# Banded attention and a feed-forward block: a second place for float32 queries and keys, and new due times for the attention units

## The chip, the core and the metric

The kernel runs on one core of a Trainium2 chip as one program. The metric is the device time of one execution in microseconds; of the kernel before there are three runs with a median of 982.79 us, and one more execution taken by the hardware profiler. Most executions of one kernel agree within 0.3%.

## The reference

Eight batches of 576 positions, eight heads of 64. Heads 0 to 3 attend to the 32 positions up to their own, heads 4 to 7 to every fourth of the 128 positions up to their own. The attention's output is then normalised, multiplied up to 2048 columns, clipped at zero, multiplied back to 512 and added to what went in:

```python
scores = np.where(masks, (q @ k.T) / 8, -1e9)      # two bands, by head
attn = exp(scores - max); attn /= attn.sum(-1) + 1e-9
x = (attn @ v) as (batch, seq, 512)
xn = (x - mean) / sqrt(var + 1e-6) * g
out = x + maximum(xn @ w1, 0) @ w2                  # 512x2048, 2048x512
```

## The kernel before, in words

**Tiles and blocks.** The 4608 rows are 36 tiles of 128 rows; three tiles make a block, and there are twelve blocks. Tiles 0 to 3 go through an early form of attention in float32, while the weights are still being loaded. Every later tile t goes through these units, each with a letter in the plan:

- L, `load_tile`: queries and keys as float32 into `qk32` (two DMAs of 512 KB, since each half of the partitions gets its own copy, L179) and values into `v32` (L187). Both places are single (`bufs=1`).
- A, `attn_prep`: splits the float32 values into a high and a low float16 part: casts on ACT (L301, L272, L151) and subtractions on POOL (L302, L273) and on DVE (L152). The halves lie in a `slot`, one of five equal places of 8 KB per partition (`SLOTS`, L245) that the raw weights and the early values use as well. A tile's slot is read until the value products of the tile after it (L513 takes `old`).
- S, `attn_scores`: 24 matmuls (L323), eight for the plain heads, then sixteen for the dilated ones, with the mask added by DVE between them (L341, L355), since `ps_s` is a single place in PSUM.
- M, `attn_softmax`: maximum on DVE (L437), subtraction on POOL (L439), two exponentials on ACT (L444, L445), the low part on POOL (L446), 18 transposes on DVE (L451, L425, L427, L428).
- V, `attn_values`: 40 matmuls (L521; 24 in a tile that begins a batch), then 1/sum and the output x on DVE (L527, L531, L533).
- N and T: mean and variance on DVE (L542), the power on POOL (L547), the normalised tile on DVE (L556), its two halves on ACT and POOL (L561, L562), and two transposing DMAs (L569) into the block's `xT`. There are two of these, one of which lies in the tile `w1_sb`: in the profile it is called `xT` for even blocks and `w_sb` for odd ones.

**The feed-forward block** (`ffn`). "Up" are 16 groups of 12 matmuls with 384 columns (L590), each ended by a clip on ACT (L596) and a difference on DVE (L597); "down" are three tiles of 48 matmuls with 512 columns (L613), each ended on DVE (L619) and by a DMA to the output (L627). Blocks 0 and 1 are worked tile by tile with matmuls of 128 columns. A block's first up matmul needs the T of all its three tiles.

**What sets the order.** All work of all tiles is cut into units with a due time. A unit may not be due before those it is built on, a table (`MOVED`) sets some times by hand, and the units are written out sorted by due time (L834). For tiles from 6 on, the time of A is `t_at = max(t_at + GAP, start - AHEAD - PER_TILE * (NB - 1 - i))`, where `start` is the time of the tile's block: `AHEAD` says how long before its block the last tile of it is prepared. S, M, V and T follow A by 6, `SOFTMAX`, `VALUES` and `READY`, and L follows the A of the tile before. The layer that records the program then keeps each engine's instructions in about that order, but lets one go ahead that it takes to be ready sooner. What stands on an engine is run in that order: an instruction that waits holds up all behind it on its engine. All DMAs are issued by SP, in one queue, and a DMA that waits for its place to become free holds up those behind it too.

Of the kernel before, what the change touches and what calls it, by code (L numbers as in the profile page):

```python
# [10 lines left out]
F32 = mybir.dt.float32  # L11
# [6 lines left out]
P = 128  # L18
H = 8
HP = 4  # L20
D = 64
# [10 lines left out]
NQK = 2 * HP * P  # L32
NBLK = NT // NB
EARLY = 4
AHEAD = 45.0
GAP = 10.0
SOFTMAX, VALUES, READY = 10.0, 20.0, 28.0
CW, SLOTS = 2, 5
HG = 4
SUMS = 128  # L40
# [7 lines left out]
}  # L48

MOVED = {  # L50
# [6 lines left out]
}  # L57
APART = 2

# [7 lines left out]
def attention_then_ffn(ctx: ExitStack, tc, qkv, masks, g, w1, w2, out):  # L67
# [3 lines left out]
    work = ctx.enter_context(tc.tile_pool(name="work", bufs=2))  # L71
# [87 lines left out]
    def after_weights():  # L159

        raw = state.get("raw")
        return nullcontext() if raw is None else tc.issue_after(raw)

    def load_tile(t):
        with after_weights() if t < NB * 2 else nullcontext():
            load_tile_now(t)

    def load_tile_now(t):
        if t == 0:
            state["early"] = work.tile([P, 2, 2, HP, P], F32, name="qk32", bufs=1)  # L170
        if t < EARLY:
            qk32 = state["early"][:, t % 2]
            nc.sync.dma_start(out=qk32, in_=qkv[t, :, 0:NQK])
            q32, k32 = qk32[:, 0], qk32[:, 1]
        else:
            qk32 = work.tile([P, 2, 2, HP, P], F32, name="qk32", bufs=1)
            src = qkv[t, :, 0:NQK].rearrange("(a d) e -> d a e", a=2)
            for on in (slice(0, D), slice(D, P)):
                nc.sync.dma_start(out=qk32[on].rearrange("d a x h c -> d a (x h c)"), in_=src)  # L179
            q32, k32 = qk32[:, :, 0], qk32[:, :, 1]  # L180
        if t < EARLY:
            v32 = slot().bitcast(F32)[:, 0 : 16 * (D + 1)]
            state[t] = dict(q32=q32, k32=k32, v32=load_ranges(t, v32))
        else:
            v32 = work.tile([P, H, D], F32, name="v32", bufs=1)
            v_in = qkv[t, :, NQK:].rearrange("p (h d) -> p h d", h=H)
            state["load", t] = nc.sync.dma_start(out=v32, in_=v_in).ins  # L187
            state[t] = dict(q32=q32, k32=k32, v32=v32)
# [54 lines left out]
    def slot():  # L243

        return work.tile([P, CW * DM * 2], I32, name="slot", bufs=SLOTS)  # L245

    def room_of(t):

        st = state[t]
        x = slot().bitcast(F16)  # L250
        at = 0
        for name, *shape in (("qs", H, P), ("khp", HP, W + P), ("klp", HP, W + P), ("khd", HP, P), ("kld", HP, P), ("vl", H, D)):
            n = shape[0] * shape[1]
            st[name] = x[:, at : at + n].rearrange("p (h c) -> p h c", h=shape[0])
            at += n
# [26 lines left out]
    def split_last(t):  # L282

        st = state[t]
        st["v32"] = work.tile([P, H, D], F32, name="v32", bufs=1)
        nc.sync.dma_start(out=st["v32"], in_=qkv[t, :, NQK:].rearrange("p (h d) -> p h d", h=H))
        for x in pt_a + pt_d:
            nc.gpsimd.memset(x, 0.0)
        room_of(t)
        kh, kl = st["khp"], st["klp"]  # L290
        halves_of(st["k32"], kh[:, :, W:], kl[:, :, W:])
        st.update(kh=kh, kl=kl)
        prep_v(t)
# [441 lines left out]
    units = {}  # L735

    def unit(name, when, what, *after):

        when = MOVED.get(name, when)
        for a in after:  # L740
            if a in units:
                when = max(when, units[a][0] + 0.001)
        units[name] = (when, len(units), what)
        return when

    PER_TILE = 24.0
    for fg in range(NKC):
        unit(f"C{fg}", TIMES["C"][fg], lambda fg=fg: prep_w1(fg), f"C{fg - 1}")
        unit(f"s{fg}", TIMES["C"][fg] + 5.0, lambda fg=fg: split_w1(fg), f"C{fg}", f"s{fg - 1}")
# [10 lines left out]
    for b in range(NBLK):  # L760
        blk = dict(t0=b * NB, b=b)
        for i in range(NB):
            t = b * NB + i
            if t < EARLY:
                t_at = TIMES["E"][t]
                if t:
                    unit(f"L{t}", t_at - 8.0, lambda t=t: load_tile(t), f"V{t - 2}")
                else:
                    unit("L0", 0.5, load_first)
                for n, (name, what) in enumerate((  # L770
                    ("S", scores_early), ("M", softmax_early), ("V", values_early), ("N", norm),
                )):
                    unit(f"{name}{t}", t_at + 3.0 * n, lambda t=t, what=what: what(t), f"L{t}", f"{name}{t - 1}")
                unit(
                    f"T{t}", t_at + 10.0, lambda t=t, i=i, blk=blk: transposes(t, blk, i), f"N{t}",
                    f"P{NFC // NW2 - 1}" if b else None,
                )
                if t == EARLY - 1:
                    unit(f"A{t}", TIMES["X"], lambda t=t: split_last(t), f"v{t}", f"N{t}")
                continue  # L780
            if t - EARLY < len(TIMES["t"]):
                t_at = TIMES["t"][t - EARLY]
            else:
                t_at = max(t_at + GAP, start - AHEAD - PER_TILE * (NB - 1 - i))

            def do(name, when, what, *after):
                return unit(f"{name}{t}", t_at + when, lambda t=t: what(t), f"{name}{t - 1}", *after)

            unit(f"L{t}", units[f"A{t - 1}"][0] + 1, lambda t=t: load_tile(t), f"A{t - 1}")


            t_at = do("A", 0, attn_prep, f"L{t}", f"V{t - 2}")
            if t % TPP == 5 and t + 4 < NT:
                do("v", 2, scale_later, f"A{t}")
            do("S", 6, attn_scores, f"A{t}")
            do("M", SOFTMAX, attn_softmax, f"S{t}", f"V{t - 1}")
            do("V", VALUES, attn_values, f"M{t}")
            do("N", VALUES + 2, norm, f"V{t}")
            unit(
                f"T{t}", t_at + READY, lambda t=t, i=i, blk=blk: transposes(t, blk, i),  # L800
                f"N{t}", f"P{NFC // NW2 - 1}" if b else None, f"b{b - 2}",
            )
        ups, downs = ffn(blk, b < APART)
        if b < APART:
            for i in range(NB):
                t = b * NB + i
                when = TIMES["U"][t] if t < len(TIMES["U"]) else start
                for fq in range(NKC):
                    us = ups[(4 * i + fq) * 4 // HG : (4 * i + fq + 1) * 4 // HG]
                    when = unit(  # L810
                        f"U{t}.{fq}", when, lambda us=us: [what() for _, what in us],
                        f"T{t}", f"s{fq}", f"U{t}.{fq - 1}", f"U{t - 1}.{fq}", f"D{t - 1 - i}.{fq}",
                    )
                    when += sum(took for took, _ in us)
                if b == 0:
                    when = TIMES["D"] + 10.4 * i
                for p in range(NKC):
                    took, what = downs[4 * i + p]
                    when = unit(
                        f"D{t}.{p}", when, what,  # L820
                        f"P{(4 * p + 3) // NW2}", f"U{t}.{p}", f"D{t}.{p - 1}", f"D{t - 2}.3" if p == 0 else None,
                    )
                    when += took
                start = max(start, when) if b else start
            last = tuple(f"D{t}.{NKC - 1}" for t in range((b + 1) * NB))
            units[f"b{b}"] = (max(units[a][0] for a in last), len(units), lambda: None)
        else:
            when = max(start, units[f"T{b * NB + NB - 1}"][0] + 0.1, max(units[a][0] for a in last))
            for n, (took, what) in enumerate(ups + downs):
                name = f"b{b}" if n == len(ups) + len(downs) - 1 else f"b{b}.{n}"  # L830
                when = unit(name, when, what, f"T{b * NB + NB - 1}", f"b{b}.{n - 1}", *last) + took
            last = (f"b{b}",)
            start = max(start + PER_TILE * NB, when)
    for _, _, what in sorted(units.values(), key=lambda e: e[:2]):  # L834
# [72 lines left out]
```

## Time and profile before

| | |
|---|---|
| three runs, median (lowest, highest) | 982.79 us (981.22, 983.58) |
| the profiled execution, its time | 991.04 us |
| its span, first to last instruction | 989.3 us |
| busy: PE, DVE, POOL, ACT | 910.8, 640.4, 313.3, 311.1 us |
| mean granted TensorE clock | 0.974 |
| HBM traffic over the span | 82 GB/s |

PE is TensorE's matmuls, PEld its weight loads, DVE VectorE, ACT ScalarE, POOL GpSimd, SP the engine that issues the DMAs. Times in the profile are microseconds from the first instruction. The granted clock is a share of full speed. A row of the groups or of the timeline has the line of the code, the engine, the operation, the tile written and the tiles read, and how many. In a row of the windows, each engine has its busy time in that stretch with its instructions in brackets, then come the clock and the DMA engines' share. Matmuls are pipelined, so "busy" says that PE had work, not that it was fast. A number in square brackets is idle time before an instruction, with what ended it.

### The profile page before, as it was taken

To read this page: it belongs to the slowest core of one execution; us is meant where nothing else is said; L and a number is where in the kernel's file an instruction comes from. 1 tells how busy PE (TensorE), PEld (TensorE's weight loads), DVE (VectorE), ACT (ScalarE), POOL (GpSimd) and SP (SyncE) were. 2 spreads that over 40 slices of the span, in tenths; PEclk is the share of its full clock that TensorE was granted. 3 is DMA by queue.
4 is the path that set the end of the run, shared out by engine and by line. 5 is a ranking of instruction groups with operands and counts; after the bars stand their busy time and mean duration, and the time that the engine had idled before them with its cause. 6 is when DMAs were issued, how large, how long until landed. Compare 5 with 4: busy or idle time off the path is not lost.

```text
span 989.3 us, 18584 instructions
## 1 busy us (share of the span) xinstructions
PE 910.8 (92%) x7608; PEld 561.4 (57%) x7608; DVE 640.4 (65%) x1379; ACT 311.1 (31%) x588; POOL 313.3 (32%) x319
## 2 busy tenths in 40 slices
PE   4497887979999999899899899899999899999998
PEld 3387564777564655555565565465565465555553
DVE  4897648697575686675675685585585595585210
ACT  3655733242231531232231441141231241130110
POOL 1101454554233153253343162262432352120000
PEclk9998899989999999999999999999999999999999
DMA  7976654745514553252422642433703331200000
GB/s 231 353 230 151 161 121 109 131 77 119 100 31 94 136 111 65 57 117 64 103 51 59 163 102 54 76 76 67 142 13 86 77 68 34 46 17 28 22 1 32
DMA packets 79622, 93.39 MB, mean 94 GB/s; under 512 B 47920, under 2 KB 53680, under 8 KB 79536
## 3 DMA queue, kind: packets, MB, share of 16 engines
q1 hardware_dynamic: 79536, 92.21, 39.9%
q8 instruction: 59, 0.97, 0.4%
q14 instruction: 27, 0.22, 0.1%
HBM read 71.86 MB, written 9.44 MB: 82 GB/s over the span
## 4 chain that ended last, share of the span: by engine, by line
PE 55%; DMA 14%; DVE 11%; POOL 8%; ACT 6%; issue 4%; SPq 1%; POOLq 0%; ACTq 0%; DVEq 0%
PE ps_f L613 28%; PE ps_f L590 22%; DMA qk<-in_qkv 6%; POOL slot L273 3%; PE ps_v L521 3%; PE ps_s L323 3%; DVE pt_d L428 2%; POOL slot L302 2%; DMA xT<-xh 2%; DMA slot<-in_w 2%; DVE pt_a L425 1%; DMA v<-in_qkv 1%; DVE sc L355 1%; POOL pk L446 1%; DVE hl L597 1%
## 5 line engine op out<-in xcount | busy, mean ns | idle before, releaser
L590 PEld LDWEIGHTS <-w_sb 128*128 128x128 f16 x3072 | 264.4, 102 | 154.2 <-issue 13.9
L613 PE MATMUL ps_f<-w_sb,hh 128*128 128x512 f16 x1152 | 346.7, 381 | 3.5 <-ACT w_sb L151 3.2
L590 PE MATMUL ps_f<-xT,w_sb 128*128 128x384 f16 (+1 forms) x1536 | 206.7, 296 | 15.3 <-DMA xT<-xh 15.0
L613 PE MATMUL ps_f<-w_sb,hl 128*128 128x512 f16 x576 | 219.3, 381 | 0.0
L590 PE MATMUL ps_f<-w_sb 128*128 128x384 f16 (+1 forms) x1536 | 204.1, 295 | 8.0 <-DMA w_sb<-xh 7.7
L613 PEld LDWEIGHTS <-hh 128*128 128x128 f16 x1152 | 112.1, 98 | 129.8 <-issue 5.8
L596 ACT ACTIVATE hh<-ps_f 128x384 f16<-128x384 f32 (+1 forms) x184 | 91.1, 501 | 224.7 <-PE ps_f L590 224.4
L597 DVE SCALAR_TENSOR_TENSOR hl<-ps_f,hh 128x384 f16<-128x384 f32 (+1 forms) x184 | 101.6, 571 | 91.6 <-ACT hh L596 89.9
L613 PEld LDWEIGHTS <-hl 128*128 128x128 f16 x576 | 56.5, 98 | 66.5 <-issue 1.9
L273 POOL TENSOR_TENSOR slot<-qk,slot 128x512 f16<-128x512 f32 x65 | 85.1, 1325 | 22.0 <-ACT slot L272 19.5
L302 POOL TENSOR_TENSOR slot<-qk,slot 64x1024 f16<-64x1024 f32 x32 | 68.2, 2130 | 63.4 <-ACT slot L301 63.3
L428 DVE STREAM_TRANSPOSE pt_d<-pk 32x256 f32<-32x256 f32 x128 | 79.5, 621 | 1.9
L355 DVE TENSOR_TENSOR sc<-ps_s,mask 32x256 f32<-32x256 f32 x128 | 53.7, 419 | 41.4 <-PE ps_s L323 39.1
L439 POOL TENSOR_TENSOR sc<-sc,mx 128x512 f32<-128x512 f32 x32 | 33.4, 1043 | 143.6 <-DVE mx L437 139.2
L301 ACT CAST slot<-qk 128x1024 f16<-128x1024 f32 x32 | 33.5, 1046 | 141.4 <-PE ps_v L521 92.7
L619 DVE SCALAR_TENSOR_TENSOR row<-ps_f,s,x 128x512 f32<-128x512 f32 x36 | 27.0, 750 | 71.2 <-PE ps_f L613 70.9
L323 PE MATMUL ps_s<-slot 128*128 128x128 f16 (+1 forms) x768 | 59.8, 227 | 9.3 <-DVE sc L355 5.1
L341 DVE TENSOR_TENSOR sc<-ps_s,mask 32x256 f32<-32x256 f32 x128 | 53.6, 418 | 20.3 <-PE ps_s L323 18.9
L323 PEld LDWEIGHTS <-slot 128*128 128x128 f16 x768 | 51.6, 100 | 20.8 <-POOL rstd L547 5.2
L280 POOL COPY slot<-slot 128x128 f16<-128x128 f16 x56 | 18.1, 346 | 136.8 <-PE ps_v L521 136.8
L562 POOL TENSOR_TENSOR xl<-xn,xh 128x512 f16<-128x512 f32 x36 | 42.3, 1176 | 56.3 <-ACT xh L561 46.4
L446 POOL TENSOR_TENSOR pk<-p,pk 128x512 f16<-128x512 f32 x32 | 40.7, 1272 | 51.5 <-ACT pk L445 51.4
(96 smaller groups left out, 847.7 us busy)
## 6 DMA issues: line engine op xcount, KB each, us to landing
qk<-in_qkv SPq DMA_DIRECT2D x68, 512.0 KB, 6.5
slot<-in_w SPq DMA_DIRECT2D x14, 1024.0 KB, 7.2
out_x<-row SPq DMA_DIRECT2D x36, 256.0 KB, 2.1
row<-in_qkv SPq DMA_DIRECT2D x33, 256.0 KB, 2.9
v<-in_qkv SPq DMA_DIRECT2D x33, 256.0 KB, 2.9
slot<-in_w SPq DMA_DIRECT2D x4, 512.0 KB, 8.5
slot<-in_qkv SPq DMA_DIRECT2D x28, 64.0 KB, 3.8
v_b<-vh SPq DMA_DIRECT2D x58, 16.2 KB, 1.8
```

The lines of the kernel that those rows point to most:

```text
L273: nc.gpsimd.tensor_tensor(out=lo, in0=x32, in1=hi, op=ALU.subtract)
L302: nc.gpsimd.tensor_tensor(out=qsv[D:P], in0=st["q32"][D:P], in1=qsv[D:P], op=ALU.subtract)
L323: nc.tensor.matmul(out, lhs, rhs, start=(n == 0), stop=(n == len(terms) - 1))
L341: nc.vector.tensor_tensor(out=sc[pj, 0:HP, :], in0=ps[pj, :, W * j : W * j + 2 * W], in1=mask_16[pj, m : m + 1, :].broadcast_to([W, HP, 2 ...
L355: nc.vector.tensor_tensor(out=sc[pj, HP:H, :].rearrange("p h (t i) -> p h t i", t=2), in0=ps[pj].rearrange("p h (t c) -> p h t c", t=2)[:, ...
L428: nc.vector.transpose(dd[pj].rearrange("p t h (i r) -> p r t h i", r=DIL)[:, j], pk[pj, HP:H, :].rearrange("p h (t i) -> p t h i", t=2),)
L446: nc.gpsimd.tensor_tensor(out=pk16[:, :, :, 1], in0=p32, in1=pk16[:, :, :, 0], op=ALU.subtract)
L562: nc.gpsimd.tensor_tensor(out=xl, in0=xn, in1=xh, op=ALU.subtract)
L590: nc.tensor.matmul(z[:, n], l, r, start=(m == 0), stop=(m == len(mm) - 1))
L596: nc.scalar.activation(hh, z, AF.Relu)
L597: nc.vector.scalar_tensor_tensor(out=hl, in0=z, scalar=0.0, in1=hh, op0=ALU.max, op1=ALU.subtract)
L613: nc.tensor.matmul(o, l, r, start=(f == 0 and m == 0), stop=(f == NFC - 1 and m == 2))
```

## The change

It has three parts.

1. Queries and keys of odd tiles (from tile 5) are loaded into a `slot` instead of `qk32`, so float32 queries and keys have two places in turn; no place is added for them. `v32` has two places (the pool's default) instead of one.
2. L is due 12.6 before the A of the tile before, instead of 1 after it, and may now stand ahead of that A (it follows the A of two tiles back).
3. The planner's numbers are others: A is due 64.3 instead of 45 before its block and successive A at least 17.2 instead of 10 apart; the softmax is due right behind the scores (0.9 is raised to S's time), the values 23 instead of 20 behind A, a tile's period is 21.7 instead of 24. A new table `MOVED` goes with them (a line of it below).

Each instruction is still there once, with the same shapes: PE has 13,991 rows in both programs.

```diff
-AHEAD = 45.0
-GAP = 10.0
-SOFTMAX, VALUES, READY = 10.0, 20.0, 28.0
+AHEAD = 64.3
+GAP = 17.2
+SOFTMAX, VALUES, READY = 0.9, 23.0, 21.7
+LOAD = -12.6
+PER_TILE = 21.7
...
 MOVED = {
-    "A5": 105.8, "A11": 227.2, "D0.2": 121.5, "D1.2": 112.6, "D1.3": 120.1, "D2.3": 139.5,
...
+    "D1.2": 113.9, "D2.3": 139.5, "D3.0": 136.5, "D4.0": 181.3, "D5.0": 202.4, "D5.1": 210.6,
...
-            qk32 = work.tile([P, 2, 2, HP, P], F32, name="qk32", bufs=1)
+            if t % 2:
+                qk32 = slot().bitcast(F32).rearrange("p (a x h c) -> p a x h c", a=2, x=2, h=HP)
+            else:
+                qk32 = work.tile([P, 2, 2, HP, P], F32, name="qk32", bufs=1)
...
-            v32 = work.tile([P, H, D], F32, name="v32", bufs=1)
+            v32 = work.tile([P, H, D], F32, name="v32")
...
-        st["v32"] = work.tile([P, H, D], F32, name="v32", bufs=1)
+        st["v32"] = work.tile([P, H, D], F32, name="v32")
...
-    PER_TILE = 24.0
...
-            unit(f"L{t}", units[f"A{t - 1}"][0] + 1, lambda t=t: load_tile(t), f"A{t - 1}")
+            unit(f"L{t}", units[f"A{t - 1}"][0] + LOAD, lambda t=t: load_tile(t), f"A{t - 2}")
```

What this does to the order is shown at two places on SP, whose queue the other engines wait for. (In the program after, a line number is 6 or 7 higher: the loads of queries and keys are L179 before and L186 after, the transposing DMAs L569 and L576, the outputs L627 and L634.)

The first place is the end of block 6 and the beginning of block 7, about 605 to 630 us in the profile of before. On SP, before; `xh_7379` and `xl_7380` are the halves of tile 23, the last of block 7, and the three outputs are those of tiles 18, 19 and 20, that is, of block 6:

```order
L627 DMA out_x<-row_7284 128x512
L627 DMA out_x<-row_7395 128x512
L240 DMA v_b1_83<-vh1_87 32x260 x2
L240 DMA v_b1_83<-slot_7619 32x4x64
L187 DMA v32_7651<-in_qkv 128x512
L179 DMA qk32_8224<-in_qkv 64x2x1024 x2
L569 DMA_TRANSPOSE w1_sb_98<-xh_7379 128x4x128
L569 DMA_TRANSPOSE w1_sb_98<-xl_7380 128x4x128
L627 DMA out_x<-row_7503 128x512
```

On SP, after; tile 23 is now `xh_7279` and `xl_7280`, the outputs of tiles 18, 19 and 20 are rows 7426, 7551 and 7665, and `xh_7535` and `xl_7536` are those of tile 24, of block 8:

```order
L576 DMA_TRANSPOSE w1_sb_98<-xh_7279 128x4x128
L576 DMA_TRANSPOSE w1_sb_98<-xl_7280 128x4x128
L634 DMA out_x<-row_7426 128x512
L194 DMA v32_7896<-in_qkv 128x512
L634 DMA out_x<-row_7551 128x512
L186 DMA slot_8194<-in_qkv 64x2x1024 x2
L576 DMA_TRANSPOSE xT_99<-xh_7535 128x4x128
L576 DMA_TRANSPOSE xT_99<-xl_7536 128x4x128
L634 DMA out_x<-row_7665 128x512
```

The transposes of block 7's last tile stood behind two of the three outputs of block 6; now they stand ahead of all three, and those of the first tile of block 8 stand ahead of the last output of block 6. On PE the same shift reads so, counted in the built programs: between the last value matmul of tile 23 and the first up matmul of block 7 there were 47 down and 24 score matmuls; now there are 144 down, 36 up, 48 score and 40 value matmuls. For the other blocks from 3 on there were 44 to 68 down matmuls in between, and now there are 120 or 144.

The second place is the beginning of the later form of attention. On SP, before, from the load of tile 5's queries and keys to that of tile 8 (`row` with `in_qkv` are values of later tiles, read only for their sum of squares; `w1_sb_98<-xh_1419` and `xl_1420` are tile 3):

```order
L179 DMA qk32_1494<-in_qkv 64x2x1024 x2
L218 DMA row_1550<-in_qkv 128x512
L218 DMA row_1553<-in_qkv 128x512
L218 DMA row_1556<-in_qkv 128x512
L179 DMA qk32_1526<-in_qkv 64x2x1024 x2
L627 DMA out_x<-row_1724 128x512
L569 DMA_TRANSPOSE w1_sb_98<-xh_1419 128x4x128
L569 DMA_TRANSPOSE w1_sb_98<-xl_1420 128x4x128
L179 DMA qk32_2099<-in_qkv 64x2x1024 x2
L627 DMA out_x<-row_2023 128x512
L179 DMA qk32_2499<-in_qkv 64x2x1024 x2
```

On SP, after, the same four loads (tiles 5, 6, 7 and 8 in turn):

```order
L186 DMA slot_1460<-in_qkv 64x2x1024
L576 DMA_TRANSPOSE xT_99<-xl_1408 128x4x128
L186 DMA slot_1460<-in_qkv 64x2x1024
L247 DMA v_b2_84<-slot_1592 32x4x64
L194 DMA v32_1662<-in_qkv 128x512
L225 DMA row_1625<-in_qkv 128x512
L225 DMA row_1628<-in_qkv 128x512
L186 DMA qk32_1522<-in_qkv 64x2x1024 x2
L225 DMA row_1631<-in_qkv 128x512
L186 DMA slot_1659<-in_qkv 64x2x1024 x2
L186 DMA qk32_2200<-in_qkv 64x2x1024 x2
```

Tiles 5 and 7 go to a slot, 6 and 8 to `qk32`, and the loads of tiles 6, 7 and 8 stand almost in a row, where before an output and tile 3's transposes stood between them.

10 rows, old and new, of the table MOVED are left out of this document.

## The prediction, made before the changed kernel was run

> **What bounds the kernel now.** I read the page first, then the busy time by stretches, then the waits, then the timeline at the waits. The page says that TensorE (PE) is the engine with the least room:
>
> ```profile
> PE 910.8 (92%) x7608; PEld 561.4 (57%) x7608; DVE 640.4 (65%) x1379; ACT 311.1 (31%) x588; POOL 313.3 (32%) x319
> ```
>
> A share of the span hides where the rest lies, so I cut the span into stages. Columns: length, busy time of PE, PEld, DVE, ACT, POOL, then the granted clock and the DMA share.
>
> ```profile
> ...
> 100.00:136.00 36.00, 29.00 (x245) 17.61 (x243) 19.05 (x37) 23.02 (x50) 17.84 (x15) 0.89 0.62 152
> 136.00:255.00 119.00, 106.25 (x1253) 80.63 (x1252) 91.07 (x198) 40.18 (x65) 62.06 (x60) 0.93 0.57 110
> 255.00:325.50 70.50, 70.50 (x504) 40.02 (x502) 42.38 (x92) 17.33 (x31) 21.67 (x22) 1.00 0.39 78
> 325.50:923.00 597.50, 575.98 (x4190) 329.28 (x4190) 399.35 (x896) 170.05 (x318) 199.10 (x196) 0.98 0.34 74
> 923.00:985.00 62.00, 62.00 (x337) 32.73 (x335) 11.19 (x19) 7.86 (x16) 0.00 (x0) 1.00 0.04 13
> ```
>
> I take as lost in a stage its idle PE time plus (1 − clock) × length. The stage 255 to 325.5 is block 2 with its three tiles of attention: 70.5 us, nothing lost. Blocks 3 to 10 take 597.5 us, of which 597.5 − 576.0 = 21.5 are idle and 0.02 × 597.5 = 12.0 go to the clock: 33.5 us, or 4.2 a block (8 × 70.5 = 564 says the same). The stage 136 to 255, mostly blocks 0 and 1, loses 12.8 + 0.07 × 119 = 21 us; 100 to 136 loses 7 + 4 = 11 us. The last block loses nothing. DVE is busy for 399 of 597 us (67%) in the steady stage, POOL for a third: neither is a bound there.
>
> The steady loss has a name in the waits (total us, times, longest):
>
> ```profile
> PE ps_f L590 <- DMA xT<-xh: 15.0, 6, 5.0
> PE ps_f L590 <- DMA w_sb<-xh: 7.7, 3, 4.2
> PEld L521 <- DVE pt_a L427: 11.4, 10, 4.0
> ```
>
> The first up matmuls of a block wait for the transposed tile; so do those of blocks 4 to 9, six times, from the first row here to the last, 15.2 us in all:
>
> ```profile
> 401.33 2.10 PE L590 MATMUL ps_f<-xT,w_sb 128*128 128x384 f16 x6 [3.25 <-DMA xT<-xh]
> ...
> 779.52 1.88 PE L590 MATMUL ps_f<-w_sb 128*128 128x384 f16 x7 [2.72 <-DMA w_sb<-xh]
> ```
>
> Block 7 shows the chain behind it, from the end of tile 23's value products to the first up matmul:
>
> ```profile
> 613.12 0.19 PE L521 MATMUL ps_v<-vh,pt_d 128*128 128x65 f16 x1
> ...
> 613.36 0.23 DVE L527 TENSOR_SCALAR rs<-ps_v,sv 128x8 f32<-128x8 f32 x1 [0.70 <-PE ps_v L521]
> ...
> 615.19 2.28 DVE L152 SCALAR_TENSOR_TENSOR slot<-v,sv,vh 128x512 f16<-128x512 f32 x1
> ...
> 619.55 0.55 POOL L547 TENSOR_TENSOR rstd<-rstd,mhalf 128x1 f32<-128x1 f32 x1
> ...
> 623.24 1.21 SPq L569 DMA_TRANSPOSE w_sb<-xl  x1
> ...
> 629.07 1.15 PE L590 MATMUL ps_f<-w_sb 128*128 128x384 f16 x5 [4.16 <-DMA w_sb<-xh]
> ```
>
> From 613.3 to 629.1 are 15.8 us. Between the two, PE had 47 down matmuls and 24 score matmuls. The last blocks give the rate of the long matmuls, 31.20 / 192 = 162 ns for up and 31.09 / 144 = 216 ns for down; score matmuls go at 1.07 / 16 = 67 ns, and a tile's V takes 1.23 us:
>
> ```profile
> 343.76 1.07 PE ps_s L323 x16
> ...
> 385.91 1.23 PE ps_v L521 x40
> ...
> 923.10 31.20 PE ps_f L590 x192
> 954.30 31.09 PE ps_f L613 x144
> ```
>
> So the cover is 47 × 0.216 + 24 × 0.067 = 11.8 us, and 15.8 − 11.8 = 4.0 is the wait of 4.16.
>
> A wait costs more than itself. The clock of the stretch after block 7's wait, of that after a wait of 1.67 us at 488, and of that with a wait of 1.66 us at 867:
>
> ```profile
> 490.00:495.00 5.00, 5.00 (x28) 2.74 (x27) 4.39 (x13) 0.98 (x2) 0.55 (x1) 0.66 0.00 0
> 630.00:635.00 5.00, 5.00 (x22) 2.64 (x21) 0.72 (x2) 1.67 (x3) 0.12 (x1) 0.67 0.00 0
> 865.00:870.00 5.00, 3.33 (x47) 2.51 (x44) 4.83 (x13) 1.22 (x2) 0.00 (x0) 1.00 0.01 3
> ```
>
> The first two lose (1 − 0.66) × 5 = 1.7 us more. The third, with its wait of 5.00 − 3.33 = 1.67 us, loses no more.
>
> The stage 136 to 255 loses to the single place for queries and keys. The chain that ended last shows the loop: a load, its casts, its subtractions, and only then the next load.
>
> ```profile
> 162.24 7.13 DMA qk<-in_qkv
> 171.06 1.71 POOL slot L302
> 172.84 2.60 POOL slot L273 x2
> 176.17 8.06 DMA qk<-in_qkv
> ```
>
> A turn takes 176.2 − 162.2 = 14 us. It hurts where the engines that wait for a load hold up other work:
>
> ```profile
> 197.60 1.05 ACT L301 CAST slot<-qk 128x1024 f16<-128x1024 f32 x1 [7.11 <-DMA qk<-in_qkv]
> 199.31 2.15 DVE L152 SCALAR_TENSOR_TENSOR slot<-v,sv,vh 128x512 f16<-128x512 f32 x1 [5.27 <-ACT vh L151]
> 204.23 1.23 PE L323 MATMUL ps_s<-slot 128*128 128x160 f16 x8 [5.09 <-DVE sc L355]
> ```
>
> ACT waits 7.1 us for tile 10's load, DVE 5.3 us for ACT, and PE 5.1 us for a mask that stands behind it on DVE.
>
> **The change, part by part.**
>
> *Attention begun sooner.* Nothing is added or removed; instructions move. In blocks 4 to 11 there are 36 or 33 up (12 in block 4) and 144 down matmuls between the last tile's V and the first up matmul: for block 7 144 × 0.216 + 36 × 0.162 + 48 × 0.067 + 1.2 for another tile's V = 41 us of cover against a chain of 15.8. Block 3 has 30 (120 down, 47 score, one V), block 2 has 20.5. The waits for T go, with their clock. What is late next is V itself, the third row of the waits. It needs the softmax: after the end of S, 11.3 us when nothing is in the way (tile 17), and 14.2 in tile 18, where the end of S is at 474.13:
>
> ```profile
> 445.36 1.06 PE L323 MATMUL ps_s<-slot 128*128 128x128 f16 x16
> 457.08 0.63 DVE L428 STREAM_TRANSPOSE pt_d<-pk 32x256 f32<-32x256 f32 x1
> 473.07 1.06 PE L323 MATMUL ps_s<-slot 128*128 128x128 f16 x16
> 488.36 0.20 PE L521 MATMUL ps_v<-vh,pt_a 128*128 128x65 f16 x1 [1.67 <-DVE pt_a L427]
> ```
>
> In the new order V stands 11.8 to 12.8 us of PE work behind the end of S, in all steady blocks. The 11.3 of tile 17 fits; V also begins with the parts that are transposed first. Bounds for the new loss: nothing, or 14.2 − 12.3 = 1.9 us in each of 23 tiles. I take the nearer row, tile 17's, for most: on POOL the subtraction of the softmax (L439) now stands behind the preparation that its own tile needed anyway, while in tile 18 it stood behind the next one's. That leaves some 4 of the 33.5 us (half a microsecond a block): **−29 us**.
>
> *Two places in turn, loads sooner.* No DMA more or less, 512 KB each as before. In the startup, the load of tile 5 need not wait until POOL has done with tile 4, and so on: each comes about one loop, 14 us, sooner, so ACT no longer waits in front of other work. Of the 21 us between 136 and 255, those behind a load are the waits in these two stretches and their clock:
>
> ```profile
> 160.00:180.00 20.00, 14.71 (x179) 12.30 (x178) 17.39 (x40) 4.72 (x8) 11.90 (x14) 0.83 0.58 132
> 200.00:220.00 20.00, 15.77 (x215) 14.38 (x216) 19.25 (x41) 7.38 (x13) 10.58 (x11) 0.83 0.51 95
> ```
>
> 5.3 + 3.4 + 4.2 + 3.4 = 16 us. Bounds for the gain: none, or all 21. New waits can come: with attention ahead, the mask for one tile stands behind another's transposes on DVE, and block 2 has only 20.5 us of cover. I count one wait of 1 to 2 us with part of its clock against it: **−14 us**. In the steady stage the loads are early either way. SP's queue is the danger of the step: a load that waits for its slot holds up transposes and outputs behind it. Five slots hold a tile's halves for about two tiles, so three or four are in use and one is left for the load; the outputs behind it have two places to write from.
>
> *Begin, 0 to 136, and end.* The weights stand on SP in the same order. The two waits there:
>
> ```profile
> 104.69 1.01 PE L613 MATMUL ps_f<-w_sb,hh 128*128 128x512 f16 x2 [3.19 <-ACT w_sb L151]
> ...
> 134.22 0.38 PE L223 MATMUL ps_v<-v_tot,ones 128*128 128x1 f32 x2 [3.50 <-DVE v_tot L221]
> ```
>
> Tile 4's and 5's preparation now lies among the splits of the second weights, and 71 down matmuls stand in a row behind those splits; against that, the second wait, for the sums of squares, may go, since their rows are read sooner. I take zero, from −3 to +5. *Second place for `v32`*: the load stands off the path; zero.
>
> **Sum.** 991.0 − 29 − 14 = 948 us for the profiled execution. It is 0.84% above the median of the three runs, so the median falls to 982.8 × 948 / 991 = 940 us.
>
> **A rule of the skill.** The waits that I leave are of 1 to 2 us, and the rows are at odds on what follows such a wait: 1.7 us of half clock after the one at 488, none after the one at 867. The Trainium skill, "TensorE: Matmul & The Clock Gate", section "What's actually happening" of its part 1, has the clock halved only after an idle window of about 3.4 us. By that rule such a wait costs only itself, and the sum is some 2 us lower, 938; the row at 490 speaks against it.
>
> **The rivals.**
>
> 1. *The slots are no second place.* The five are full, the odd loads wait for a V as before for POOL, and the startup keeps its 21 us; the change then does only half of what it says. For it: weights, early values and halves share them just then. Against: tile 5's load stands in the new order as soon as its slot is free of weights. 982.8 − 29 = 954 us.
> 2. *V in place of T.* V waits in every steady tile because 12.3 us are too few. At 1.9 us and 1.7 us of clock in 23 tiles it costs 83 us; the T part of the 33.5 us is gone (six block starts, 15.2 us of waits and 10.2 of clock, 25), the startup's 14 too: 982.8 − 39 + 83 = 1027 us. It decides from 39 / 23 = 1.7 us a tile on. For it: tile 18's row. Against: tile 17's, and POOL's new order. By the Trainium skill's rule above the waits would not halve the clock, and this rival would end at 982.8 − 39 + 44 = 988 us.
> 3. *V waits a little*, some 0.8 us a tile without clock: 940 + 0.8 × 23 = 958 us.
> 4. *Nothing to speak of*: gains and new waits even out within 0.2%, about what a measurement of this kernel can tell from no change.
>
> **Chances.** Forecast 0.62; rival 1 0.19; rival 3 0.11; rival 2 0.05; rival 4 0.03. Faster by over 0.2% is 0.62 + 0.19 + 0.11 = 0.92, the same 0.03, slower 0.05. The range begins where all 33.5 + 21 us and the 3 of the beginning go (982.8 − 57 = 926) and ends with rival 3 and some loss at the start (962); it leaves out rivals 2 and 4 and the worst of 3.
>
> **What would show it.** Right: no row in the waits with PE waiting for `xT<-xh` or `w_sb<-xh` from block 3 on; the stage of blocks 3 to 10 at a clock of 1.00 and about 568 us long; block 2's first up matmul about 10 us sooner with a tile more of attention done; ACT's waits for `qk` gone between 136 and 255. Wrong: `L521 <- DVE` as the largest wait of PE (rival 2 or 3); PE's waits for L323 between 136 and 255 as long as now (rival 1); a first down matmul much later than 104.7 us (the beginning).

## The result, and the profile after

The kernel after takes 943.62 us (median of 4 runs, 942.53 to 945.08) against 983.18 us (981.22 to 986.83) for the kernel before, measured beside it: a ratio of 0.9594, 95% interval 0.9563 to 0.9626. The forecast was 940, in a range from 926 to 962. The profiled execution after took 944.02 us (span 942.2) where that of before took 991.04.

The page of after, busy time by engine: TensorE has lost 20 us of busy time with the same instructions, because more of them ran at the full clock.

```profile
PE 890.7 (95%) x7608; PEld 552.2 (59%) x7608; DVE 634.2 (67%) x1379; ACT 312.7 (33%) x588; POOL 312.3 (33%) x319
```

The stretches of after (columns as in the prediction; the granted clock is the third number from the end):

```profile
140.00:300.00 160.00, 158.28 (x1679) 108.09 (x1677) 128.83 (x293) 53.07 (x89) 75.73 (x74) 1.00 0.50 99
300.00:340.00 40.00, 36.45 (x258) 21.18 (x257) 24.71 (x62) 15.99 (x37) 11.65 (x11) 0.97 0.44 114
340.00:877.00 537.00, 537.00 (x3963) 309.35 (x3962) 370.74 (x824) 155.63 (x282) 192.91 (x188) 1.00 0.35 74
```

From 340 us to the end of block 10 TensorE is never idle and never slowed: 537.00 of 537.00 at 1.00. The startup, 140 to 300 us, loses 1.7 us. What is lost in between, 300 to 340 us, is 3.6 us idle and 0.03 × 40 = 1.2 of clock; it was not foreseen.

The waits of TensorE in after that answer to those shown of before:

```profile
PE ps_f L620 <- ACT w_sb L153: 5.0, 1, 5.0
PE ps_v L230 <- DVE x L486: 4.6, 1, 4.6
...
PE ps_f L597 <- DMA xT<-xh: 2.4, 2, 1.8
...
PE ps_v L230 <- DVE v_tot L228: 2.1, 1, 2.1
```

The wait for transposed tiles is 2.4 us in two places instead of 22.7 in nine. The timeline of after at block 7: the values of tile 23 end at 558.4, its second transpose is issued at 567.7, and the block's first up matmul starts nearly 32 us later without any wait.

```profile
558.19 0.20 PE L528 MATMUL ps_v<-vh,pt_d 128*128 128x65 f16 x1
...
567.68 1.27 SPq L576 DMA_TRANSPOSE w_sb<-xl  x1
...
599.28 0.98 PE L597 MATMUL ps_f<-w_sb 128*128 128x384 f16 x5
```

To compare many kernels I use one measure. I let each matmul count its usual rate (162 ns an up, 216 a down, 56 or 69 a score matmul, 28 to 32 a value matmul, and so on for the others) and call **lag** the time at which a matmul starts minus the sum of the rates of all matmuls before it. It grows by every wait and by every stretch at a lower clock, and does not depend on what order the work has. All are from the profiled executions, one of each kernel. That of before lay 4 to 8 us above the medians of before, that of e11 4 us below its own and the others within 3 us of theirs, so differences of a few us say nothing by themselves. Each kernel was measured beside runs of before; medians are compared through the ratios.

| kernel | lag at 140 us | 140 to 300 | 300 to the end | median, us | ratio to before (95%) |
|---|---|---|---|---|---|
| before | 64.6 | 19.4 | 37.8 | 983 to 987 | 1 |
| after | 64.4 | 3.1 | 8.1 | 943.6 | 0.9594 (0.9563 to 0.9626) |
| e1: places and loads alone | 66.7 | 8.6 | 44.6 | 985.9 | 0.9993 (0.9963 to 1.0023) |
| e8: places alone, loads late | 58.7 | 15.0 | 46.1 | 990.4 | 1.0059 (1.0037 to 1.0081) |
| e11: e1, two tiles' keys later | 63.5 | 8.0 | 38.2 | 981.9 | 0.9945 (0.9926 to 0.9965) |
| e2: order alone | 63.0 | 24.3 | 14.8 | 971.1 | 0.9845 (0.9804 to 0.9885) |
| e6: after, one place for v32 | 60.5 | 13.3 | 7.3 | 949.6 | 0.9641 (0.9613 to 0.9669) |
| e7: after, loads late | 61.1 | 7.1 | 14.9 | 951.7 | 0.9662 (0.9641 to 0.9682) |
| e3: after, 19 units later | 62.5 | 4.2 | 24.1 | 959.7 | 0.9730 (0.9689 to 0.9771) |
| e12: e3, two tiles' keys later | 62.1 | 4.4 | 16.0 | 951.9 | 0.9648 (0.9615 to 0.9680) |
| e4: after, 29 units later | 59.7 | 17.4 | 68.1 | 1013.6 | 1.0279 (1.0227 to 1.0332) |
| e5: after, sums 18 units later | 63.8 | 3.5 | 14.7 | 949.8 | 0.9641 (0.9619 to 0.9663) |
| e13: after, sums 31 units later | 63.0 | 3.2 | 11.6 | 947.8 | 0.9609 (0.9572 to 0.9646) |
| e10: after, rows spread | 61.4 | 12.6 | 8.8 | 949.8 | 0.9626 (0.9612 to 0.9640) |

Before and after differ by −0.2, −16.3 and −29.7 us in the three stages.

### The profile page after: what moved, and what is told of

Same layout as the page of the kernel before. It is cut to its first block, busy times and chain, and to the rows that moved or that the text cites. A ratio compares the mean times of both kernels' runs of the same rounds, so it can differ in the third digit from the quotient of the medians.

```text
span 942.2 us, 18610 instructions
## 1 busy us (share of the span) xinstructions
PE 890.7 (95%) x7608; PEld 552.2 (59%) x7608; DVE 634.2 (67%) x1379; ACT 312.7 (33%) x588; POOL 312.3 (33%) x319
## 4 chain that ended last, share of the span: by engine, by line
PE 81%; DMA 10%; ACT 3%; DVE 3%; issue 2%; SPq 1%; POOL 1%; ACTq 0%; DVEq 0%; POOLq 0%
PE ps_f L597 36%; PE ps_f L620 35%; PE ps_s L330 4%; PE ps_v L528 4%; DMA row<-in_qkv 4%; DMA slot<-in_w 3%; DMA xT<-xl 1%; ACT row L226 1%; DMA slot<-in_qkv 1%; DMA v<-in_qkv 0%; PE ps_f L673 0%; ACT w_sb L153 0%; DVE slot L662 0%; POOL slot L280 0%; DVE slot L154 0%
## 5 line engine op out<-in xcount | busy, mean ns | idle before, releaser
L597 PEld LDWEIGHTS <-w_sb 128*128 128x128 f16 x3072 | 256.0, 99 | 126.6 <-issue 4.6
L597 PE MATMUL ps_f<-xT,w_sb 128*128 128x384 f16 (+1 forms) x1536 | 199.2, 289 | 2.9 <-DMA xT<-xh 2.4
L597 PE MATMUL ps_f<-w_sb 128*128 128x384 f16 (+1 forms) x1536 | 196.7, 287 | 0.0
L451 ACT ACTIVATE p<-sc 128x512 f32<-128x512 f32 x32 | 20.2, 631 | 128.2 <-POOL sc L446 128.2
L569 POOL TENSOR_TENSOR xl<-xn,xh 128x512 f16<-128x512 f32 x36 | 42.0, 1166 | 59.1 <-ACT xh L568 49.8
L330 PE MATMUL ps_s<-slot 128*128 128x128 f16 (+1 forms) x768 | 58.8, 226 | 2.1 <-DVE sc L348 2.1
L330 PEld LDWEIGHTS <-slot 128*128 128x128 f16 x768 | 50.9, 99 | 12.7 <-DVE sc L348 3.0
L458 DVE STREAM_TRANSPOSE pt_b<-pk 32x128 f16<-32x128 f16 x87 | 26.1, 300 | 42.0 <-ACT pk L452 28.4
L554 POOL TENSOR_TENSOR rstd<-rstd,mhalf 128x1 f32<-128x1 f32 x36 | 21.1, 587 | 94.9 <-DVE rstd L553 85.2
```

The lines of the kernel that those rows point to most:

```text
L330: nc.tensor.matmul(out, lhs, rhs, start=(n == 0), stop=(n == len(terms) - 1))
L569: nc.gpsimd.tensor_tensor(out=xl, in0=xn, in1=xh, op=ALU.subtract)
L597: nc.tensor.matmul(z[:, n], l, r, start=(m == 0), stop=(m == len(mm) - 1))
```

## The experiments

The theory to be tried was that of the prediction: the steady gain comes from the order (the transposes of a block's last tile are issued well ahead), the startup's from the places, and each would come without the other.

### Each half alone

**Places and loads alone (e1).** The kernel before with:

```
+            if t % 2:
+                qk32 = slot().bitcast(F32).rearrange("p (a x h c) -> p a x h c", a=2, x=2, h=HP)
+            else:
                 qk32 = work.tile([P, 2, 2, HP, P], F32, name="qk32", bufs=1)
...
-            v32 = work.tile([P, H, D], F32, name="v32", bufs=1)
+            v32 = work.tile([P, H, D], F32, name="v32")
...
-            unit(f"L{t}", units[f"A{t - 1}"][0] + 1, lambda t=t: load_tile(t), f"A{t - 1}")
+            unit(f"L{t}", units[f"A{t - 1}"][0] - 12.6, lambda t=t: load_tile(t), f"A{t - 2}")
```

> The two places and the sooner loads alone, with the planner's numbers of before. Theory (the moved order gives the steady gain of some 30 us, the places the startup's 16): 983 - 16 = 967 us, from 962 to 972; the waits for the transposed tile at the starts of blocks 4 to 9 stay at some 15 us in all, and the stage from block 2's start to block 11's is as long as before. Rival A (the places carry the gain, since later loads are late everywhere): 943 to 950. Rival B (the five slots are no second place): 983.

Measured: 985.87 us, ratio 0.9993: nothing. That is near the time of rival B, but not for its reason, as the lag shows: the places do their work in the startup. **Order alone (e2)** is the kernel after with the reverse of this diff, so with the new table of numbers, one place each and the late loads.

> The planner's new numbers alone, with one place for queries and keys, one for the values, and loads behind the preparation of the tile before. Theory: the steady gain stays and the startup's goes, 944 + 16 = 960 us, from 952 to 964; no wait for the transposed tile from block 3 on, ACT's waits for queries and keys between 136 and 255 us back at several us each. Rival A (the places carry the gain): 975 to 983. Rival B: 944, the same as with both.

Measured: 971.11 us, ratio 0.9845 (0.9804 to 0.9885), a gain of 15 us and not the 23 expected, between the ranges of the theory and of rival A. So nothing and −15 alone, −40 together: the halves do not add. The lag shows that each half does what it was said to do in its stage, and that the other stage then takes it back: e1 loses 8.6 us instead of 19.4 in the startup, but 44.6 instead of 37.8 later; e2 loses 14.8 instead of 37.8 later, but 24.3 in the startup, more than before.

What holds e2 up is in its waits (ScalarE's wait for the queries' load, in total, times, longest) and in its timeline at two places:

```profile
ACT slot L303 <- DMA qk<-in_qkv: 46.2, 10, 8.6
```

```profile
178.64 1.04 ACT L303 CAST slot<-qk 128x1024 f16<-128x1024 f32 x1 [7.16 <-DMA qk<-in_qkv]
...
180.63 1.07 ACT L598 ACTIVATE hh<-ps_f 128x512 f16<-128x512 f32 x2
...
181.28 1.03 PE L615 MATMUL ps_f<-w_sb,hh 128*128 128x512 f16 x2 [4.29 <-ACT hh L598]
```

ScalarE stands 7.2 us in front of a load; the ReLU behind it comes late, and TensorE's down matmul waits 4.3 us for it. The other place is at 455 us:

```profile
454.77 0.69 DVE L439 TENSOR_REDUCE mx<-sc 128x8 f32<-128x512 f32 x1
455.17 1.04 ACT L303 CAST slot<-qk 128x1024 f16<-128x1024 f32 x1 [4.81 <-DMA qk<-in_qkv]
...
456.35 2.13 POOL L304 TENSOR_TENSOR slot<-qk,slot 64x1024 f16<-64x1024 f32 x1 [4.69 <-ACT slot L303]
458.55 2.27 POOL L275 TENSOR_TENSOR slot<-qk,slot 128x512 f16<-128x512 f32 x2
...
460.77 1.04 POOL L441 TENSOR_TENSOR sc<-sc,mx 128x512 f32<-128x512 f32 x1
```

The maximum of the softmax is there at 455.5, but GpSimd stands in front of the next tile's halves until 460.8, and the values of this tile come 15.6 us after its scores instead of 12.4; TensorE waits 1.1 us for them. That is the mechanism of the prediction's rival 2, and the single place feeds it. In after, ScalarE's waits for these loads are 0.2 us (`qk`) and 1.9 us (`slot`) in all.

### What the places run into in the old order

e1 waits 6.73 us at the start of block 5, where before waited 0.81. Before, at the second transpose of tile 17 and at the block's first up matmul:

```profile
471.32 1.21 SPq L569 DMA_TRANSPOSE w_sb<-xl  x1
...
474.94 0.34 PE L590 MATMUL ps_f<-w_sb 128*128 128x384 f16 x1 [0.81 <-DMA w_sb<-xh]
```

e1, the same place (L565 makes the low half `xl`, L305 and L276 the halves of tile 19's queries and keys):

```profile
459.67 2.13 POOL L305 TENSOR_TENSOR slot<-slot 64x1024 f16<-64x1024 f32 x1
...
462.19 2.27 POOL L276 TENSOR_TENSOR slot<-slot 128x512 f16<-128x512 f32 x2
...
464.42 1.15 POOL L565 TENSOR_TENSOR xl<-xn,xh 128x512 f16<-128x512 f32 x1
...
465.49 1.26 SPq L182 DMA_DIRECT2D slot<-in_qkv  x2
466.85 1.23 SPq L572 DMA_TRANSPOSE w_sb<-xl  x1
...
475.57 0.80 PE L593 MATMUL ps_f<-w_sb 128*128 128x384 f16 x2 [6.73 <-DMA w_sb<-xl]
```

Now that tile 19's queries are there in time, GpSimd makes its halves first; the low half of tile 17 comes behind them, its transpose is issued 14.4 us after the end of the values (10.9 in before), and behind a load of two times 512 KB on the same queue the up matmuls that need it start 8.7 us after that. In before, the block's first up matmul came 3.6 us after the issue. (In e1 four up matmuls, which need only the high half, had run at 466.1.) The transposes of tile 26, in front of block 8, go the same way (13.6 us). Two experiments ask which of the two it is.

**Places, loads late (e8):** e1 with the last line of its diff undone.

> The kernel before with two places for queries, keys and values, and the loads where they were. Theory (the places win 10 us before 320 us; with the earlier loads the later blocks lost 7 us of it again because 1 MB of loads then stood beside the transposes that the short cover of the old order waits for): 976 us, 972 to 981, with the first ups of blocks 5 and 8 waiting less than in the run with earlier loads (6.7 and 3.8 us). Rival (the earlier load is itself what the startup gains from, and the transposes were late for another reason): 983 to 988.

Measured: 990.35 us, ratio 1.0059 (1.0037 to 1.0081). My theory fell, and the time is above the rival's range too. The wait at block 5 is shorter than in e1 (two, of 1.4 and 3.3 us), but that at block 8 is longer (4.8). With late loads the chain is long at four block starts (4, 5, 6 and 8) instead of two, since GpSimd gets to the next tile's halves just when a tile's values have ended: at block 4 it makes them from 383.2 us on, and the low half stands behind them at 387.9.

**Two tiles' keys later (e11).** e1 with tile 19's and 28's halves tied behind the low halves of tiles 17 and 26 (their A also follows the N of those tiles in the order of units):

```
+KEYS_LATER = (19, 28)
...
     def attn_prep(t):
-        prep_stacked(t)
+        if t in KEYS_LATER:
+            with tc.issue_after(state["xl", t - 2]):
+                prep_stacked(t)
+        else:
+            prep_stacked(t)
```

> The run with the places alone, in which GpSimd's key halves of tiles 19 and 28 are put behind the low half of the normalized tiles 17 and 26, whose transposes open blocks 5 and 8. Theory (with two places those key halves come ready in time to stand ahead of the low half, and TensorE waits 6.7 and 3.8 us longer at these two block starts, with a low clock behind each): 975 us, 970 to 979, and both second transposes issued 11 us after the values' end instead of 14. Rival (the transposes are late through the loads on the DMA engines): 983 to 988, unchanged.

Measured: 981.85 us, ratio 0.9945 (0.9926 to 0.9965), just above the range of the theory and below that of the rival. The timeline of e11 at the same place:

```profile
458.61 1.26 SPq L577 DMA_TRANSPOSE w_sb<-xl  x1
...
464.56 1.11 PE L598 MATMUL ps_f<-w_sb 128*128 128x384 f16 x4 [3.86 <-DMA w_sb<-xh]
```

The transpose is issued 11.7 us after the values (10.0 at block 8), but a load of two times 512 KB is still in front of the two transposes on the queue, and the block starts 6 us later, not 3.6. So both are at work. From the end of the values to the up matmuls that wait there are 14.6 us in before, 23.1 in e1 and 17.6 in e11: the order on GpSimd, with what it moves on the queue, is the larger part of what e1 lost at this place. The lag from 300 us on is 38.2, near that of before. With that, part of the startup's gain of the places stays, 5 us by the ratio.

### How much cover is needed

**Attention 19.3 units later (e3)** and **29.3 later (e4)**: after with one number.

```
-AHEAD = 64.3
+AHEAD = 45.0
```

> The changed kernel with attention due 45 instead of 64.3 before its block, as in the kernel before; the other numbers stay new. In the built program the cover between a block's last value products and its first up matmul is 18.1 us of TensorE work (20 in blocks 2 and 3), against 41 in the changed kernel and 11.6 before. Theory (what counts is only whether the cover is over the chain of 14 to 16 us): 944 us, from 942 to 950. Rival (every us of lead helps, or the number itself carries the gain): halfway or all the way back, 960 to 973.

> The same with attention due 35 before its block: the cover is 9.0 to 9.9 us in blocks 2 and 4 to 10, 11.9 in block 3, 7.2 in block 11. Theory: each block from 2 on waits 15.8 - 9.2 = 6.6 us and loses 1.7 us more to the clock, ten times: 944 + 83 = 1027 us, from 1005 to 1035, with waits for the transposed tile of over 50 us in all. Rival (lead counts in proportion): about 990. Rival (the places carry the gain): 944 to 955.

e4 (the same line with 35.0) took 1013.57 us, ratio 1.0279 (1.0227 to 1.0332), inside the theory's range and 13 us below its sum: with 9 us of work between a block's last values and its first up matmul, the old waits are back and larger. But they are 38.7 us in all, where the theory had over 50, and TensorE also waits for masks (the row of L330). Waits of e4:

```profile
PE ps_f L597 <- DMA xT<-xh: 17.5, 7, 5.2
PE ps_f L597 <- DMA w_sb<-xh: 15.9, 4, 6.2
...
PE ps_s L330 <- DVE sc L362: 10.4, 5, 3.2
...
PE ps_f L597 <- DMA xT<-xl: 4.3, 4, 3.3
...
PE ps_f L597 <- DMA w_sb<-xl: 1.0, 2, 0.5
```

e3 took 959.70 us, ratio 0.9730 (0.9689 to 0.9771), where the theory said 944 and a rival 960 to 973. The chain of 15.8 us that I had read in before is not the longest. In block 5 of e3, where the values end at 438.8:

```profile
453.76 1.23 SPq L576 DMA_TRANSPOSE w_sb<-xl  x1
...
462.80 0.64 PE L597 MATMUL ps_f<-w_sb 128*128 128x384 f16 x2 [4.85 <-DMA w_sb<-xl]
```

The chain of tile 17, up to the up matmuls that need its low half, is 24.0 us with the two places, for the reason seen in e1. **e12** is e3 with the edit of e11:

> The changed kernel with the attention begun 19.3 units later (as in the run with 45 units, 959.7 us), and the key halves of tiles 19 and 28 behind the low half of tiles 17 and 26. Theory (18 us of cover is enough for the chain of a tile, 15.8 us, and what was lost there were two block starts at which the key halves lengthen the chain, 14 us with the low clock behind them): 947 us, 942 to 952. Rival (the new order needs more than 18 us of cover in any block): 957 to 962, unchanged.

Measured: 951.92 us, ratio 0.9648 (0.9615 to 0.9680), in the theory's range and outside the rival's. The wait at block 5 is gone. Of the 1.4% that e3 stands above after, 0.6% remains, among it a wait of 3.2 us inside block 6, for the low half behind a ReLU. So 18 us of cover did for most blocks, and the worst would have needed 24; what the 41 us of the new order give beyond that was not tried. Nor was `AHEAD` tried alone: which of the planner's other numbers the steady gain also needs is open.

### The smaller parts

**One place for v32 in after (e6)**, with `bufs=1` put back in two lines, and **late loads in after (e7)**, with the load's line put back:

> The changed kernel with one place for the float32 values again, the two places for queries and keys and the earlier loads kept. Theory (the second place for values is worth nothing): 944 us, 941 to 948. Rival (with one place the earlier load of the values waits on SyncE for the tile before, and the queries and keys of the tile behind it in the queue with it): 955 to 971, the time with all places single.

> The changed kernel with the places kept but the loads put where they were, one unit behind the preparation of the tile before. Theory (the place counts, since a load into it no longer waits for the float32 keys to be read; where the load stands in the program counts little, as 20 us lie between two preparations and a load lands in 5 to 8): 946 us, 942 to 952. Rival (the places do nothing by themselves and the 12.6 units are the gain): 965 to 975, as with the plan alone (971).

e6: 949.55 us, ratio 0.9641 (0.9613 to 0.9669), so 0.5% above after, with intervals that overlap by a little, and between the ranges of the theory and the rival; one wait of 9 us in the startup is where the profile shows it:

```profile
PE ps_v L230 <- DVE v_tot L228: 11.2, 2, 9.0
```

e7: 951.73 us, ratio 0.9662 (0.9641 to 0.9682), 0.7% above after and in the theory's range. Of the 25 us that e2 lacks to after, the early load and the second `v32` cost some 7 and 5 when taken away by themselves. The other 13 would be the places for queries and keys if the parts added; these places were not taken away by themselves.

### The sums of squares

Three runs went after what after still loses: the two waits for the sum over partitions (L230), at 132.5 and 336.6 us. **e5** splits `scale_v` behind the squares and puts the second part, with the sum, into a unit of its own; **e13** writes 33 for the 20 in this line, which puts the sum between the values of two tiles:

```
+                do("z", 20, scale_end, f"v{t}")
```

> The changed kernel with the two halves of the value scales apart: loads and squares where they were, the sum over partitions (L230) 18 time units later, so that TensorE no longer meets it before the squares are done. Theory (what is left between 100 and 340 us is this sum: 4.6 us of wait at 132.5, 2.05 at 336.6, and the low clock behind each): 936 us, 932 to 940, and neither wait in the profile. Rival (the wait only hides others, of the same tile's values or of the first downs, which end no sooner): 941 to 946.

> The changed kernel with the sum of each later value scale 31 time units behind the loads and squares, which puts it between the values of two tiles: the one accumulator for values is free then, the squares are long done, and the values of tile 13 no longer stand behind the sum. Theory (the 5 to 6 us that the order of after loses between 320 and 360 us are the sum's place ahead of the values of tile 13, and the 4.6 us at 132 are its place ahead of the squares): 936 us, 931 to 940, with tile 13's values starting 12 to 14 us behind its scores instead of 37. Rival (ScalarE still stands still for the rows, and its next work, of whatever kind, is late by as much): 943 to 950.

e5: 949.77 us; e13: 947.78 us (942.71 to 950.44), ratio 0.9609 (0.9572 to 0.9646), not to be told from after. **e10** loads and squares one row every five units instead of nine in a row:

> The changed kernel with the nine rows of each later value scale loaded and squared one at a time, five time units apart, and the sum over partitions 7 units behind the last: ScalarE then waits for no queue of rows, and VectorE's sum of the squares no longer stands ahead of the early values' division and the masks. Theory (what is left between 100 and 340 us comes from ScalarE waiting 4 to 5 us for a row, whichever engine then shows it): 937 us, 933 to 941, with no wait for the sum over partitions. Rival (the rows' loads only meet other loads, or the sum now holds TensorE's values of a later tile in the one accumulator): 943 to 952.

e10: 949.77 us. None is what the theory said: e13 and e10 lie in the ranges of their rivals, and e5 lies above both. The wait for the sum at 132 us is gone, and another, larger one stands in its place (7.5 us in e5, 6.0 in e13, 6.1 in e10). In after, the sum was late since ScalarE waited for a row, and VectorE for ScalarE (TensorE's wait is put down to L486, the division of the early values, which stands behind the sum on VectorE):

```profile
130.35 0.63 ACT L226 ACTIVATE row<-row 128x512 f32<-128x512 f32 x1 [5.28 <-DMA row<-in_qkv]
...
131.10 0.16 DVE L228 TENSOR_REDUCE v_tot<-v_sums 128x1 f32<-128x9 f32 x1 [4.37 <-ACT row L226]
...
132.51 0.54 PE L230 MATMUL ps_v<-v_tot,ones 128*128 128x1 f32 x2 [4.61 <-DVE x L486]
```

In e13 there is no sum at this place any more on TensorE, but VectorE takes it up as early as before, and the mask behind it is late:

```profile
126.91 0.63 ACT L226 ACTIVATE row<-row 128x512 f32<-128x512 f32 x1 [5.85 <-DMA row<-in_qkv]
...
127.67 0.16 DVE L231 TENSOR_REDUCE v_tot<-v_sums 128x1 f32<-128x9 f32 x1 [4.94 <-ACT row L226]
...
130.61 1.89 PE L337 MATMUL ps_s<-slot 128*128 128x128 f16 x16 [5.96 <-DVE sc L355]
```

In e10 the row that ScalarE waits for is at 180 us, and TensorE waits at 186.5 for the ReLU behind the rows. In after the row itself is late for two reasons. It is issued only at 123.4 us, when ScalarE has squared the row whose place it takes (`row` has two places). And the DMA engines are full: between 118 and 130 us its 256 KB took 6.8 us to land beside four DMAs of 512 KB, those of two tiles' queries and keys, against a median of 2.9 over the program. These two rows are of after's view of the DMA engines in that stretch, the queue (packets, MB, share of 16 engines) and the issues:

```profile
q1 hardware_dynamic: 1170, 2.71, 95.9%
...
row<-in_qkv SPq DMA_DIRECT2D x1, 256.0 KB, 6.8
```

I had blamed the place of the sum; these rows point to the load of the row. That is read from the profile and not shown by a run: e10, which moved the loads, met the same wait elsewhere, and no run gave the rows another place. No version of these was faster than after.

## Why the prediction was right, and where its steps were not

*Attention begun sooner, −29 us.* Measured −29.7 from 300 us on. Blocks 3 to 10 run from 313.4 to 875.9 us, 562.5 us (597.4 before, by the same two first up matmuls), at a clock of 1.00 from 340 us. Of these 34.9 us some 3.5 are attention that is now done before block 3. The waits for transposes are gone from block 3 on. The choice between tile 17's 11.3 us and tile 18's 14.2 for the softmax was right: from tile 16 on the values stand 11.6 to 12.6 us behind the scores and hardly wait, so rivals 2 and 3 fell. The 4 us that the sum left in blocks 3 to 10 for such waits were lost too (2.6 idle and 1.7 of clock), but that is luck: they lie between 320 and 341 us, most of them at a sum of squares. And the reason for the short chain was half of it. That GpSimd's subtraction stays clear of the next tile's halves is not the order's doing alone: in e2, with the order and the single place, it stood behind them (455.5 to 460.8) and values waited. "In the steady stage the loads are early either way" is the sentence that failed: the lag from 300 us on is 14.8 in e2 and 8.1 in after.

*Two places, −14 us.* Measured −16.3 from 140 to 300 us, with ScalarE's long waits for `qk` gone and block 2's first up matmul 12.3 us sooner (10 were forecast). Rival 1 (the slots are no second place) fell. The term holds only beside the order: without it the places and sooner loads win 10.8 us in that stage and lose 6.8 behind it (e1), through a chain that they themselves lengthen. That interaction was nowhere in the prediction. Its sum was right because after has both halves; it would have been wrong for either, 967 against 985.9 and 960 (as I expected of the runs) against 971.1.

*The chain of 15.8 us.* Right for block 7 of before, and taken as the chain of all blocks. With the places it is 24 us in block 5 (e3), and the 41 us of cover hide that. (The 67 ns for a score matmul were a little too long: it is busy time over 16, and by their starts these come every 56 ns.)

*Begin, 0 to 136.* Zero was right, −0.2 at 140 us. That the second wait, "for the sums of squares, may go", was wrong: it was 3.5 us and is 4.6. The first down matmul waits 5.0 us (3.2 before) and yet starts at 103.9 instead of 104.7.

*What was not foreseen:* the sum at 336.6 us, in block 3, with its wait of 2.05 us and the half clock behind it, some 4 us of lag between 320 and 341.

*The size.* By the profiled executions the change was worth 47.0 us where the sum had 43: 944.0 against 948. By the medians it was worth 39.6 where 42.8 were forecast. What put the forecast 3.6 us below the result is the step from the profiled time to the median: before's profile lay 0.84% above its median, and I took the same for after, whose profile lies only 0.4 us above it.

*The rule on the clock.* The row at 490 spoke against waits of under 3.4 us being free, and so does after; the last section says why the rows at 490 and 867 differ. These two stretches lie before and behind the wait at 336.64:

```profile
332.00:337.00 5.00, 2.95 (x19) 1.70 (x18) 2.90 (x8) 2.92 (x8) 0.90 (x1) 1.00 0.34 101
337.00:342.00 5.00, 5.00 (x23) 2.58 (x21) 2.08 (x9) 2.49 (x5) 1.41 (x2) 0.66 0.00 2
```

## What to carry to other kernels

Two halves of a change that remove different waits need not add: here a second buffer alone brought nothing, since the work that came ready sooner took its place ahead of a chain with no slack, and a new order alone brought 15 us, since engines then stood in front of the single buffer; only the two together brought 40. When a wait is cut, ask what the freed engine will do first, and who stands behind that in its queue. And before moving an instruction that waits, follow the wait to its first cause: three ways of moving a late sum won nothing, since by the profile a load in front of it was late and whatever came next paid for it.

## What the runs showed of the hardware

How long a wait must be before the clock drops can be read from the 14 profiles. Their records of the granted clock begin and end only on a grid of 3.413 us, which does not move with the waits. I cut each profile along its own grid from 145 to 900 us and took the windows at full clock, by how long TensorE was idle in them:

| idle share of a window at full clock | windows | the next one at half clock |
|---|---|---|
| under 0.5 | 2924 | 0 |
| 0.5 to 0.6 | 18 | 6 |
| 0.6 and more | 43 | 43 |

So it is not the length of a wait that counts but how much of one window is idle. The prediction's two waits of 1.67 us in before, at 488 and at 867, show it. In the window of the first, TensorE is busy for 1.62 us of 3.42, and the next one is at half clock; in that of the second it is busy for 1.75, and the next one stays at full clock:

```profile
486.57:489.99 3.42, 1.62 (x29) 1.19 (x29) 3.32 (x8) 0.00 (x0) 0.00 (x0) 1.00 0.00 0
489.99:493.40 3.41, 3.41 (x13) 1.60 (x12) 3.23 (x9) 0.49 (x1) 0.00 (x0) 0.50 0.00 0
865.45:868.87 3.42, 1.75 (x25) 1.40 (x22) 3.28 (x9) 0.95 (x2) 0.00 (x0) 1.00 0.00 0
868.87:872.28 3.41, 3.41 (x23) 2.06 (x21) 3.31 (x8) 0.76 (x2) 0.00 (x0) 1.00 0.00 0
```

A wait of 3.42 us in e1, at 625, fell into two windows, of which 0.44 and 0.56 were idle, and cost no clock. One window at half clock costs half of 3.41, the 1.7 us of the prediction's rows. The Trainium skill, "TensorE: Matmul & The Clock Gate", section "What's actually happening", has a free-running window of 3413 ns and a drop after an idle one. The traces agree with the window; a window did not have to be wholly idle here, about half of it was enough. The ends of matmuls are modelled, so the idle shares are not exact, and no run tried the bound by itself.
